# A recurrent attention with a gated feed-forward network on one core: raw weight words of the first units issued from ScalarE's queue, and the first load of x placed behind v

## The chip, the core and the metric

The kernel runs on 1 core of a Trainium2 chip. The metric is device time in microseconds (us), lower is better. Before the change it is 476.92 us (median of 3 runs, 476.25 to 478.91).

## The reference

Two blocks are computed one after the other, all in FP32 precision.

```python
# gated linear attention: B, H, S, D = 4, 8, 768, 48
for t in range(S):
    state = alpha[:, :, t, :, None] * state + einsum('bhd,bhe->bhde', k[:, :, t], v[:, :, t])
    y[:, :, t] = einsum('bhd,bhde->bhe', q[:, :, t], state)
# feed-forward: x is y as (3072, 384); w1, w2: (384, 1024); w3: (1024, 1024); w_out: (1024, 384)
a = x @ w1
b = x @ w2
out = ((a * b) @ w3) @ w_out
```

q, k, v and alpha are FP32. The four weights arrive as 64-bit floats, and the kernel reads them as raw 64-bit words and builds FP32 from them.

## The kernel before

**Chunks.** The sequence is cut into N = 24 chunks of C = 128 positions, six to a batch. A chunk n goes through these helpers, each named after what it makes:

- `load_a`, `load_kq`, `load_v` load alpha (192 KB), k and q (192 KB each) and v (192 KB). Their rows are 48 numbers, 192 bytes, long. Alpha and the pair of k and q have three buffers each, v has five.
- `logs` takes the logarithm of alpha on ScalarE (L272), `decays` sums it along the chunk on TensorE (L287) and takes two exponentials on ScalarE (L293, L294).
- `decayed` multiplies k and q by them on VectorE (L303, tile qk), `transposed` turns them on TensorE (L325) and copies them from PSUM on ScalarE (L327, tile qkT; two copies, the second is marked as ("qkT", n)).
- `scores` multiplies them on TensorE (L365) and masks the result on VectorE (L368, tile ms).
- `attend_state` (L385) and `attend` (L391) make the chunk's y on TensorE, ScalarE copies it (L395, tile x), and `store` writes it to a DRAM tensor xd on SP's queue in the next iteration (L262). `outer` (L337, then VectorE L345 or L347) and `advance` carry the state.

**Weight units.** w1 and w2 are converted in twelve units of 128 rows and 512 columns; the first six make the first half of the columns. A unit is a generator, `load_gates`, that calls `to_fp32`. Its first step loads 512 KB of raw words (L192; tile raw, four buffers, rows of 4 KB), the next ones convert: on ScalarE L200 (rest), L205 (power) and L217 (high part h), on VectorE L201, L204, L207, L208, L210 and L219 (low part l). `fetch(ahead)` takes first steps until `ahead` units are begun; `convert` does a fetch and then one further step of the oldest unit. `third` makes another part of a unit on TensorE (L233, L234) and ScalarE (L235).

**Gate.** Three chunks make a group. `load_x` reads a group's x back from xd (L407, tile xT, 576 KB), `split_x` splits it into three parts (ScalarE L413, VectorE L414 and L415), and `gate` multiplies the parts with those of the weights on TensorE (L421). The first group's split stands in iteration FIRST - 1 = 5, its matmuls begin in iteration 6. After the loop over chunks come the remaining gates, the folding of w3 with w_out, and the projection.

**What sets the order.** Each engine works through its own list in order, and so does each queue of DMA issues. Instructions are placed on the lists by the program's text and by the tile framework's scheduler; `after_marks(name)` holds what is issued inside it behind the marked instruction in that placement. Before the change all loads and stores of this stage are issued on SP's queue, the small transfers of the ends of chunks on POOL's. The transfers of SP take eight semaphores in turn, so a transfer waits for the one eight places before it to have landed; transfers issued by ScalarE take part in the same turn.

The loop over chunks begins so, before the change:

```python
    for n in range(N + 1):
        store()
        if n in loads:
            load_x(loads[n])
        load_a(n + 5)
        raws = (3, 3, 3, 3, 2, 2, 3, 3)[n] if n < 8 else 4
        for m in (n + 3,) * (n <= FIRST) + (n + 4,) * (n >= FIRST):
            load_kq(m)
            if n < FIRST - 2:
                fetch(raws)
            load_v(m - 1)
```

So the raw words of a unit lie on SP's queue between q and v of a chunk, and in iteration 4 `load_x(0)` stands behind the loads of that iteration.

Of the kernel before, what the change touches and what calls it, by code (L numbers as in the profile page):

```python
# [48 lines left out]
def kernel(  # L49
# [12 lines left out]
    nc = tc.nc  # L62
    B, H, S, D = q.shape
# [7 lines left out]
    KM = DM // C  # L71
# [31 lines left out]
    def bank():  # L103
        return ps.tile([C, 512], FP32, tag="bank", name="bank")

    st, mark = {}, {}

    def after_marks(*names):
        stack = ExitStack()
        for x in names:  # L110
            stack.enter_context(tc.issue_after(mark[x]))
        return stack
# [12 lines left out]
    def rows(src, n):  # L125
        b, c = divmod(n, NCH)
        return src[b, :, ds(c * C, C), :].rearrange("h p d -> p h d")
# [13 lines left out]
    def load_v(n):  # L141
        if n < N:
            st["v", n] = vs[n % len(vs)]
            nc.sync.dma_start(out=st["v", n][:, :, 0:D], in_=rows(v, n))

    nc.scalar.preload_act_table_set(LN_EXP_SET)
    load_a(0)
# [36 lines left out]
    for x in Ts + decs:  # L184
        nc.gpsimd.memset(x, 0.0)

    def to_fp32(dst, *srcs):

        n, m = len(srcs) * srcs[0].shape[1], srcs[0].shape[1]
        raw = rawp.tile([C, n], I64, tag="raw", name="raw")  # L190
        for i, src in enumerate(srcs):
            nc.sync.dma_start(out=raw[:, ds(i * m, m)], in_=src)  # L192
        yield
        words = raw.bitcast(U32).rearrange("p (n w) -> p n w", w=2)
        low, high = words[:, :, 0], words[:, :, 1]

        mant = cvt.tile([C, n], FP32, tag="mant", name="mant")
        top = mant.bitcast(U32)
        rest = cvt.tile([C, n], FP32, tag="rest", name="rest", bufs=2)
        nc.scalar.activation(rest, low, AF.Copy, scale=2.0 ** -52)  # L200
        nc.vector.tensor_scalar(top, high, 0x000FFFFF, 0x00100000, op0=ALU.bitwise_and, op1=ALU.bitwise_or)  # L201

        power = cvt.tile([C, n], U32, tag="power", name="power", bufs=2)
        nc.vector.tensor_scalar(power, high, 20, 0x7FF, op0=ALU.logical_shift_right, op1=ALU.bitwise_and)  # L204
        nc.scalar.activation(power, power, AF.Relu, scale=2.0 ** 23, bias=rebias)  # L205
        yield
        nc.vector.scalar_tensor_tensor(mant, top, 2.0 ** -20, rest, op0=ALU.mult, op1=ALU.add)  # L207
        nc.vector.scalar_tensor_tensor(power, high, 0x80000000, power, op0=ALU.bitwise_and, op1=ALU.bitwise_or)  # L208
        to = mant if dst is None else dst()
        nc.vector.tensor_mul(to, mant, power.bitcast(FP32))  # L210
        yield
        return to
# [24 lines left out]
    def fetch(ahead=3):  # L237
        while weights and len(begun) < ahead:
            begun.append(weights.popleft())
            next(begun[-1])  # L240
# [17 lines left out]
    def store():  # L258

        while later:  # L260
            dst, src = later.popleft()
            nc.sync.dma_start(out=dst, in_=src)  # L262
# [51 lines left out]
    def transposed(n):  # L314
        if n >= N:
            return
        qk = qks[n % 3]
        qkT = work.tile([C, 2, NP, C], FP32, tag="qkT", name="qkT")

        tp = [bank().rearrange("p (i j c) -> p i j c", i=2, j=NP) for _ in range(2)]  # L320
        for i in range(2):
            for j in range(NP):
                for half in range(2):
                    s = ds(DP * half, DP)
                    nc.tensor.transpose(tp[half][:, i, j, :], qk[s, i, 2 * j:2 * j + 2, :], ident[s, s])  # L325
        for half in range(2):
            mark["qkT", n] = nc.scalar.copy(qkT[:, :, :, ds(DP * half, DP)], tp[half]).ins  # L327
        st["qkT", n] = qkT
# [76 lines left out]
    def load_x(g, queue=nc.sync):  # L405
        st["xT", g] = xp.tile([C, KM, TG], FP32, tag="xT", name="xT")
        queue.dma_start(out=st["xT", g], in_=xd[g].rearrange("(k p) t -> p k t", p=C))  # L407
# [176 lines left out]
    with after_marks(("e", 0)):  # L584
        logs(1)
    decays(1)
    fetch(1)
    load_a(3)
    load_kq(2)
    decayed(1)  # L590
    fetch(2)
    load_v(1)
    load_a(4)


    FIRST = 6
# [3 lines left out]
    for n in range(N + 1):  # L600
        store()
        if n in loads:
            load_x(loads[n])
        load_a(n + 5)
        raws = (3, 3, 3, 3, 2, 2, 3, 3)[n] if n < 8 else 4
        for m in (n + 3,) * (n <= FIRST) + (n + 4,) * (n >= FIRST):
            load_kq(m)
            if n < FIRST - 2:
                fetch(raws)
            load_v(m - 1)  # L610
        if n:
            attend_state(n - 1)
        if n < N:
            scores(n)
        transposed(n + 1)
        if n - 2 in begin and n > FIRST:
            g, tiles = begin[n - 2]
            with after_marks(("ms", n), ("qkT", n + 1)):
                split_x(g, 0)
            fill.extend(gate(g, f) for f in tiles)  # L620
        pieces = (3, 3, 2, 0)[(n - FIRST) % 4] if n >= FIRST else 0
        if n == 0:
            with after_marks(("qkT", 0)):
                logs(2)
            decays(2)
            with after_marks(("e", 2)):
                logs(3)
        early, ready = n < FIRST, len(thirds) if n > 2 else n // 2
        marks = (*[("qkT", n + 1)] * (n < N - 1), *[("qk", n + 1), ("ms", n)] * early, *["x3"] * (n - 2 in begin and n > FIRST))
        if n < N - 2:  # L630
            with after_marks(*marks):
                convert(2 if n == 0 else 1, raws)
        advance(n)
        if n:
            attend(n - 1)
        outer(n)
        third(ready)
        run(pieces > 0)
        if early:
            with after_marks(*marks):  # L640
                convert(1, raws)
        with after_marks(*[("ms", n)] * (n < 3)):
            decayed(n + 2)
        if not early:
            with after_marks(*[("qkT", n + 1)] * (n < N - 4)):
                logs(n + 4)
        if n == 4:
            load_x(0)
        convert(early and n > 0, raws)
        run(pieces > 1)  # L650
        decays(n + 3)
        if early:
            with after_marks(("e", n + 3)):
                logs(n + 4)
        if n < N - 2:
            convert(early or n % 3 == 0, raws)
        if n == FIRST - 1:
            assert len(done) == 2 * KM
            g, tiles = begin[n - 2]
            with after_marks("l"):  # L660
                split_x(g, 0)
            fill.extend(gate(g, f) for f in tiles)
        run(pieces > 2)
        if n == N - 3:
            while begun:
                convert(1)
            weights.extend(load_out(j) for j in range(KF))
            fetch(4)
# [91 lines left out]
```

## Time and profile before

| what | value |
|---|---|
| median of the runs (range) | 476.92 us (476.25 to 478.91) |
| the profiled execution | 479.25 us |
| its span | 477.5 us |
| TensorE busy (PE) | 460.6 us, 96% |
| VectorE busy (DVE) | 359.4 us, 75% |
| ScalarE busy (ACT) | 279.4 us, 59% |
| GpSimd busy (POOL) | 71.2 us, 15% |
| raw words of w1, w2, w3 (L192), SP's queue | 28 transfers of 512 KB, median 5.3 us to landing |
| alpha, k, q, v, SP's queue | 24 transfers each of 192 KB, median 5.1, 5.2, 5.3 and 4.3 us to landing |

Every time inside the profile counts from the start of the span and belongs to the one profiled execution. Line numbers (L192) are those of the kernel before. PE is TensorE's matmul, PEld its loading of the stationary operand, SPq the queue of DMA issues of SyncE. The granted clock is TensorE's, as a share of full speed. The share of busy time over the whole span says little about the change, since it lies in the first 70 us or so; views that are cut to stretches are the ones to read.

### The profile page before, as it was taken

To read this page: it belongs to the slowest core of one execution; us is meant where nothing else is said; L and a number is where in the kernel's file an instruction comes from. 1 tells how busy PE (TensorE), PEld (TensorE's weight loads), DVE (VectorE), ACT (ScalarE), POOL (GpSimd) and SP (SyncE) were. 2 spreads that over 40 slices of the span, in tenths; PEclk is the share of its full clock that TensorE was granted. 3 is DMA by queue.
4 is the path that set the end of the run, shared out by engine and by line. 5 is a ranking of instruction groups with operands and counts; after the bars stand their busy time and mean duration, and the time that the engine had idled before them with its cause. 6 is when DMAs were issued, how large, how long until landed. Compare 5 with 4: busy or idle time off the path is not lost.

```text
span 477.5 us, 10025 instructions
## 1 busy us (share of the span) xinstructions
PE 460.6 (96%) x3836; PEld 435.6 (91%) x3836; DVE 359.4 (75%) x578; ACT 279.4 (59%) x555; POOL 71.2 (15%) x139
## 2 busy tenths in 40 slices
PE   4988899999999999999999999999999999999996
PEld 2766689889999998999999999999999999999996
DVE  2789677899969878899999968945542876666761
ACT  4668655768658554898877675654543533333330
POOL 3313112104202220112221201211011000000000
PEclk9999879999999999999999999999999999999999
DMA  9899999999899965467776532203012985555611
GB/s 170 184 205 206 226 203 264 197 220 202 191 227 202 215 190 150 130 211 227 224 243 188 172 138 84 97 37 100 33 51 70 267 244 173 167 168 173 179 51 49
DMA packets 153663, 80.29 MB, mean 168 GB/s; under 512 B 104480, under 2 KB 145696, under 8 KB 153616
## 3 DMA queue, kind: packets, MB, share of 16 engines
q1 hardware_dynamic: 148160, 65.42, 55.8%
q0 software_dynamic: 5456, 14.24, 9.3%
q8 instruction: 30, 0.49, 0.5%
q14 instruction: 17, 0.14, 0.1%
HBM read 57.58 MB, written 22.06 MB: 167 GB/s over the span
## 4 chain that ended last, share of the span: by engine, by line
PE 90%; DVE 3%; DMA 3%; ACT 2%; issue 1%; SPq 1%; DVEq 0%; ACTq 0%
PE bank L421 71%; PE bank L365 4%; PE bank L391 4%; PE bank L325 2%; PE bank L385 2%; PE bank L337 2%; PE bank L287 2%; PE bank L523 1%; DMA v<-in_v_dram 1%; PE bank L290 1%; DMA kq<-in_q_dram 1%; DVE qk L303 1%; DMA ac<-in_alpha_dram 1%; DVE power L208 0%; DVE mant L207 0%
## 5 line engine op out<-in xcount | busy, mean ns | idle before, releaser
L421 PE MATMUL bank<-x,w 128*128 128x384 f32 x1152 | 215.4, 341 | 1.1 <-ACT x L413 1.0
L421 PEld LDWEIGHTS bank<-x,w 128*128 128x128 f32 x1152 | 202.3, 190 | 4.8 <-ACT x L413 1.4
L421 PE MATMUL bank<-w3o,ab 128*128 128x384 f32 x576 | 100.2, 336 | 0.0
L421 PEld LDWEIGHTS bank<-w3o,ab 128*128 128x128 f32 x576 | 99.9, 188 | 0.0
L446 ACT ACTIVATE bank<-bank 128x384 f32<-128x384 f32 x96 | 45.7, 476 | 41.6 <-PE bank L421 41.4
L430 ACT ACTIVATE t<-bank 128x384 f32<-128x384 f32 x64 | 31.6, 495 | 63.3 <-PE bank L421 62.2
L496 POOL DMA_DIRECT2D abd<-ab x45 | 25.5, 566 | 145.1 <-DVE ab L482 126.3
L482 DVE TENSOR_TENSOR ab<-bank,r 128x384 f32<-128x384 f32 x44 | 24.4, 555 | 25.2 <-ACT bank L446 15.4
L552 DVE TENSOR_TENSOR ab<-abl,ab 128x1024 fp32r<-128x1024 f32 x24 | 29.4, 1225 | 12.8 <-ACT ab L551 12.8
L327 ACT COPY qkT<-bank 128x512 f32<-128x512 f32 x48 | 26.0, 594 | 22.0 <-PE bank L325 22.0
L551 ACT ACTIVATE ab<-abl 128x1024 fp32r<-128x1024 f32 x24 | 25.5, 1061 | 20.3 <-PE bank L421 17.9
L421 PE MATMUL bank<-wo,w3T 128*128 128x384 f32 x192 | 35.9, 334 | 0.0
L421 PEld LDWEIGHTS bank<-wo,w3T 128*128 128x128 f32 x192 | 33.5, 188 | 0.0
L368 DVE TENSOR_TENSOR ms<-bank,keep 128x512 int32<-128x512 int32 x48 | 31.3, 684 | 0.9 <-PE bank L365 0.8
L303 DVE TENSOR_TENSOR qk<-kq,e 128x768 f32<-128x768 f32 x24 | 23.2, 968 | 11.0 <-ACT e L294 8.8
L432 DVE SCALAR_TENSOR_TENSOR r<-bank,t 128x384 f32<-128x384 f32 x40 | 22.2, 555 | 12.1 <-PE bank L421 6.0
L365 PEld LDWEIGHTS bank<-qkT 48*128 48x128 f32 x384 | 24.9, 199 | 6.2 <-issue 3.4
L205 ACT ACTIVATE power<-power,rebias 128x512 uint32<-128x512 uint32 (+1 forms) x36 | 25.1, 699 | 9.0 <-DVE power L204 8.9
L432 DVE SCALAR_TENSOR_TENSOR o<-bank,t 128x384 f32<-128x384 f32 x24 | 13.4, 558 | 22.4 <-issue 13.7
L365 PE MATMUL bank<-qkT 48*128 48x128 f32 x384 | 29.7, 297 | 0.0
L553 DVE SCALAR_TENSOR_TENSOR ab<-ab,abl 128x1024 fp32r<-128x1024 f32 x24 | 29.3, 1219 | 0.0
L391 PE MATMUL bank<-ms,v 128*64 128x128 f32 x384 | 27.6, 288 | 0.0
(80 smaller groups left out, 574.9 us busy)
## 6 DMA issues: line engine op xcount, KB each, us to landing
raw<-in_moe_w_dram SPq DMA_DIRECT2D x28, 512.0 KB, 5.3
abl<-abd SPq DMA_DIRECT2D x24, 512.0 KB, 4.5
abd<-ab POOLq DMA_DIRECT2D x45, 192.0 KB, 3.1
xT<-xd POOLq DMA_DIRECT2D x9, 576.0 KB, 4.6
ac<-in_alpha_dram SPq DMA_DIRECT2D x24, 192.0 KB, 5.1
kq<-in_k_dram SPq DMA_DIRECT2D x24, 192.0 KB, 5.2
kq<-in_q_dram SPq DMA_DIRECT2D x24, 192.0 KB, 5.3
v<-in_v_dram SPq DMA_DIRECT2D x24, 192.0 KB, 4.3
```

The source lines that it names most:

```text
L303: mark["qk", n] = nc.vector.tensor_mul(qks[n % 3][:, :, :, 0:D], st.pop(("kq", n)), st.pop(("e", n)).rearrange("p i (h d) -> p i h d", h=H ...
L327: mark["qkT", n] = nc.scalar.copy(qkT[:, :, :, ds(DP * half, DP)], tp[half]).ins
L365: nc.tensor.matmul(sc[i][:, j, :], qkT[r, 0, j, :], qkT[r, 1, j, :], start=True, stop=True)
L368: masked = nc.vector.tensor_tensor(ms[:, i].bitcast(I32), sc[i].bitcast(I32), keep_bc, op=ALU.bitwise_and)
L391: nc.tensor.matmul(to, vc[:, 2 * j + i, :], ms[:, i, j, :], start=(n % NCH == 0 and j % HP == 0), stop=(j % HP == HP - 1), skip_group_chec ...
L421: nc.tensor.matmul(p, w[part][i], x[part][i], start=start and part == parts[0] and i == 0, stop=stop and part == parts[-1] and i == n - 1, ...
L430: nc.scalar.activation(t, p1, AF.Copy, scale=(1.0 + 1.0 / P) * scale)
L432: nc.vector.scalar_tensor_tensor(to, p2, scale, t, op0=ALU.mult, op1=ALU.add)
L446: nc.scalar.activation(p, p, AF.Copy, scale=1.0 + 1.0 / P)
L496: (nc.gpsimd if late else nc.sync).dma_start(out=abd[g][:, f, :], in_=ab)
L552: nc.vector.tensor_sub(t[:, 1], ab, t[:, 0].bitcast(FP32))
L553: nc.vector.scalar_tensor_tensor(t[:, 2], t[:, 0].bitcast(FP32), -1.0 - 1.0 / P, ab, op0=ALU.mult, op1=ALU.add)
```

## The change

Four things are edited.

1. `to_fp32` issues the raw words of the first 2 * KM = 6 units on ScalarE's queue; all later ones stay on SP's.
2. The fetches are placed elsewhere. The first stands behind the marked exponential of chunk 1 (it stood on SP's queue ahead of alpha of chunk 3), and `fetch(2)` before the loop is gone. In the loop, iterations 0 to 4 fetch behind the copies of qkT of chunk n + 1, where iterations 0 to 3 fetched between q and v.
3. `raws`, the number of units that may be begun, is 2 and not 3 in iterations 0 to 3.
4. `load_x(0)` in iteration 4 is held behind the last load of v.

```diff
     def load_v(n):
         if n < N:
             st["v", n] = vs[n % len(vs)]
-            nc.sync.dma_start(out=st["v", n][:, :, 0:D], in_=rows(v, n))
+            mark["v"] = nc.sync.dma_start(out=st["v", n][:, :, 0:D], in_=rows(v, n)).ins
...
+    fetched = []
+
     def to_fp32(dst, *srcs):
 
         n, m = len(srcs) * srcs[0].shape[1], srcs[0].shape[1]
         raw = rawp.tile([C, n], I64, tag="raw", name="raw")
+        fetched.append(n)
         for i, src in enumerate(srcs):
-            nc.sync.dma_start(out=raw[:, ds(i * m, m)], in_=src)
+            (nc.scalar if len(fetched) <= 2 * KM else nc.sync).dma_start(out=raw[:, ds(i * m, m)], in_=src)
         yield
...
     decays(1)
-    fetch(1)
+    with after_marks(("e", 1)):
+        fetch(1)
     load_a(3)
     load_kq(2)
     decayed(1)
-    fetch(2)
     load_v(1)
     load_a(4)
...
-        raws = (3, 3, 3, 3, 2, 2, 3, 3)[n] if n < 8 else 4
+        raws = (2, 2, 2, 2, 2, 2, 3, 3)[n] if n < 8 else 4
         for m in (n + 3,) * (n <= FIRST) + (n + 4,) * (n >= FIRST):
             load_kq(m)
-            if n < FIRST - 2:
-                fetch(raws)
             load_v(m - 1)
         if n:
             attend_state(n - 1)
         if n < N:
             scores(n)
         transposed(n + 1)
+        if n < FIRST - 1:
+            with after_marks(("qkT", n + 1)):
+                fetch(raws)
...
         if n == 4:
-            load_x(0)
+            with after_marks("v"):
+                load_x(0)
```

## The prediction

> **What bounds the kernel now.** I read the page first: TensorE (PE) is busy 96% of the span, so time can only be gained where PE idles or runs at a lower clock. The table by stretches of 10 us (columns: length, busy time of PE, weight load, VectorE, ScalarE, POOL, then PE clock, DMA share, GB/s) says where that is.
>
> ```profile
> 20.00:30.00 10.00, 9.52 (x138) 8.01 (x137) 8.47 (x15) 7.18 (x15) 3.64 (x7) 1.00 1.00 183
> 30.00:40.00 10.00, 8.58 (x122) 6.21 (x120) 8.49 (x15) 7.51 (x17) 2.17 (x4) 1.00 0.91 213
> 40.00:50.00 10.00, 7.76 (x117) 6.10 (x118) 9.17 (x17) 8.09 (x18) 2.03 (x5) 0.94 1.00 213
> 50.00:60.00 10.00, 7.97 (x89) 5.42 (x89) 6.31 (x10) 6.82 (x16) 1.88 (x3) 0.84 1.05 214
> 60.00:70.00 10.00, 9.89 (x65) 8.54 (x66) 7.17 (x13) 4.53 (x10) 1.43 (x4) 0.71 0.99 203
> 70.00:80.00 10.00, 10.00 (x140) 9.46 (x135) 9.37 (x16) 6.31 (x16) 1.72 (x3) 1.00 1.03 257
> ```
>
> The reader is to see that from 70 us on PE is full, so whatever is gained before 70 us is kept to the end, and that before it three resources are near their limit together: the DMA share is 0.9 to 1.05, VectorE is at 8.5 to 9.2 of 10, PE loses its time to both. From 20 to 60 us PE lacks 0.48 + 1.42 + 2.24 + 2.03 = 6.2 us. Next, the waits of 18 to 68 us (engine line, releaser: us in total, times, longest):
>
> ```profile
> PE bank L325 <- DVE qk L303: 3.1, 3, 1.6
> DVE qk L303 <- DMA kq<-in_q_dram: 2.2, 3, 1.2
> DVE w L219 <- ACT w L217: 2.2, 2, 1.4
> PE bank L337 <- DMA v<-in_v_dram: 2.0, 3, 1.2
> PE bank L421 <- ACT x L413: 1.0, 1, 1.0
> ```
>
> VectorE waits for q, PE for v, and PE for what VectorE makes of q. Then the timeline of SP's queue and the chain of waits, for where q and v stand and how the first gate matmul (L421) comes to start:
>
> ```profile
> 27.01 1.23 SPq L139
> 28.24 0.05 issue
> 28.29 0.99 SPq L192
> 29.28 0.04 issue
> 29.33 6.28 DMA v<-in_v_dram
> ...
> 54.32 0.69 DVE ms L368
> 55.01 0.88 DVE qk L303
> 55.88 0.14 issue
> 56.02 0.73 PE bank L325 x16
> 56.76 0.04 issue
> 56.79 1.07 ACT qkT L327 x2
> 57.87 1.07 ACT x L413
> 58.96 1.37 DVE x L414
> ```
>
> SP issues q, then raw words of a weight unit (L192), then v, and v lands 6.28 us later. The last stretch is serial: mask, qk of chunk 7, transposes, their copies, the split of x on ScalarE, the split on VectorE, and only then the gate. The xT load was issued at 50.70 and landed 5.8 later, at 56.5: it was there 1.2 us before ScalarE took it, so the order on ScalarE (behind the copies of qkT of chunk 7) set the start, not the load.
>
> [...]in slices of 1 us the granted clock is 0.50 from 49 to 52 us and 0.50 to 0.57 from 59 to 66 us[...], each after idle PE.
>
> **The change part by part.**
>
> (a) Six raw issues leave SP's queue: 1.01, 0.71, 0.78, 0.99, 0.63 and 1.68 us, 5.80 in sum, of a queue that issues without a break from 0.74 to 63 us. The instruction order of the changed kernel shows what that moves: v of chunk 3 is SP's 21st transfer and not its 25th, q of chunk 4 its 20th and not its 23rd, k, q, v of later chunks stand a group further ahead of the stores of x. So q's wait on VectorE (2.2 us, on VectorE which is 85 to 92% busy there) should go. I take 2.0. What is late next: VectorE itself. From the table its busy time between 20 and 50 us is 26.1 of 30 us, so at most 3.9 us are there to be had. The wait for v (2.0) lies on PE while VectorE was working (no gap on VectorE from 31.55 to 41.05), so its going is worth nothing by itself.
>
> (b) Each raw issue now stands on ScalarE, behind the copies of qkT and ahead of the unit's L200 and L205. ScalarE is busy 22.8 of the 30 us from 20 to 50. Per issue I take SP's mean, 5.80/6 = 0.97 us. Beside the iteration at 36 us: the copies end at 36.33, L200 would then end at 37.98 and L205 at 38.70, while VectorE took their results at 37.73 (L207) and 38.34 (L208): 0.25 to 0.36 late; in the changed order VectorE has a qk product (0.96) in between in most iterations, which hides it. I take 0.2 for each of six, 1.2 us. Below: 0, if the product always covers. Above: SP's issues of k and q took up to 3.27 us each[...]; six of these are 19.6 us against 7.2 us of free ScalarE time. The issue also waits for the transfer eight issues back; those are a chunk older and should have landed.
>
> (c) The lead of the raw words. Now a unit is issued after qkT of chunk n+1 and used one iteration later. In the timeline the copies end at 22.8, 29.0, 36.3, 42.5 and the first use on VectorE (L201) of the next unit is at 29.29, 36.61, 43.35, 49.33: a lead of 6.5 to 7.6 us against a landing of 4.8 to 6.7. It fits, with 0 to 1 us to spare if iterations shrink to VectorE's own some 6.2 us (qk 0.96, masks 2 x 0.68, T 0.35, unit 3.5). Cost taken: 0; bounds 0 to 1 us in each of five.
>
> (d) The start of the gate. In the changed order ScalarE splits x before it copies qkT of chunk 7, and VectorE makes qk of chunks 7 and 8 before it ends unit 5. That takes away PE's gap before L325 at 54.97 (1.05 us) and its wait for the split (1.0 us): 2.0 us. The xT load now stands behind one more a and k, but no raw words are in SP's queue, and the stores of x before it were held up there (x of chunk 2 was copied at 38.8, its store issued at 45.27). I take xT as landed in time; bound: 384 KB more ahead of it, at the 185 GB/s of the slices with small rows only, is 2.1 us later, which would eat it all.
>
> (e) The clock. From 58.98 to 68.09 (L365 of chunk 7) PE needed 9.1 us for 27 gate matmuls and one L287 pair; the same set at full clock, 18 in 3.41, 9 in 1.72 and the pair in 0.51, is 5.6. So 3.5 us are lost there to half clock and starts of the split. [...]Bounds 0 and 3.5; I take 1.4, a little under half[...].
>
> Sum: 2.0 + 2.0 + 1.4 - 1.2 = 4.2 us less. The profiled execution took 479.25 (span 477.5, and 1.75 around it), so it would be 475.05; the median of the runs is 476.92, so I forecast 472.7.
>
> After 70 us both kernels do the same work, and the six later units stay on SP; PE has 10.0 of 10 there, so I expect neither gain nor loss.
>
> **The rivals.**
>
> 1. Forecast, 0.45: 472.7 (469.5 to 474.5, from 2.4 to 7 us gained).
> 2. The clock stays full over the start of the gate as well: 2.0 + 2.0 + 3.5 - 1.2 = 6.3 us, 470.6. For it: five shorter gaps on PE. Against: PE's work per iteration is about 5.3 of 6.2 us. 0.15.
> 3. The transfer is the bound anyway. No byte is saved, the DMA share is about 1.0 from 2 us on, and xT has more in front of it. Then q and v come earlier only at the price of raw words and xT, and the gate starts where it did: 2 us gained early, 1 to 2 lost: 476. For it: the share. Against: the share falls to 0.3 to 0.7 in single slices (22 to 25, 34 to 36, 45 to 46, 53 to 55 us), so there is room. 0.18.
> 4. Slower: ScalarE is held at the raw issue, at L192's new place, [...]by the transfer eight back. It decides from about 1.7 us an issue, where the 1.2 us of (b) have become the 5 that are gained. At 2.5 us an issue, five issues that lie on the path at 2.5 - 0.97 + 0.2 = 1.7 each are 8.7 us, less 4 gained and with unit 5 late at the gate: 481. For it: k and q issues of 3.2 us, [...]and everything behind the issue on ScalarE (L200, L205, copies of x, the exponentials that the next qk needs) waits, with PE and VectorE behind these. Against: SP's raw issues[...] took 1.0 on average. 0.22.
>
> **How the numbers follow.** What a measurement of this kernel can tell from no change is about 0.5%, 2.4 us. Cases 1 and 2 are faster (0.60), case 3 is the same (0.18), case 4 slower (0.22). The range goes from the far side of case 2 (467.5: q's 2.2, v's 2.0, 2.0 and 3.5 in full, at no cost, are 9.7 us, to 467.2) through case 3 and into the near part of case 4 (479.5); the forecast's own range is 469.5 to 474.5.
>
> **What would show it.** Right: raw issues on ScalarE near 1 us; no wait of qk for q between 18 and 50 us; ScalarE's split of x ahead of the copies of qkT of chunk 7; the first L421 at 54 to 56 us instead of 58.98; L365 of chunk 7 at 62 to 66 instead of 68.09. Wrong: ScalarE issues of 2 us and more, or VectorE waiting at L201 for raw words, or L421 waiting for xT; and any gap of PE after 70 us would break the step that keeps the gain.

## The result and the profile after

| | before | after |
|---|---|---|
| median of 10 runs | 477.30 us | 480.13 us |
| range | 476.25 to 478.91 | 479.28 to 481.23 |
| profiled execution, its span | 479.25, 477.5 | 481.23, 479.4 |
| scores of chunk 7 on TensorE start (L365, now L368) | 68.09 | 69.92 |

The ratio is 1.0056, 95% interval 1.0041 to 1.0071: slower by about 2.7 us, where 4.2 less were forecast. Lines of the changed kernel stand three higher in number (raw words L195, rest L203, high part L220, low part L222, split of x L416 to L418, gate L424).

First the table of stretches of the changed kernel, with the columns named in the prediction.

```profile
20.00:30.00 10.00, 7.82 (x101) 6.29 (x98) 8.09 (x16) 6.11 (x14) 2.73 (x5) 0.83 1.11 191
30.00:40.00 10.00, 7.82 (x84) 6.42 (x83) 6.53 (x11) 4.96 (x11) 2.78 (x6) 0.66 0.96 187
40.00:50.00 10.00, 8.65 (x123) 6.62 (x121) 7.27 (x14) 7.23 (x17) 1.85 (x4) 1.00 0.97 203
50.00:60.00 10.00, 8.70 (x117) 6.91 (x116) 7.13 (x13) 9.19 (x20) 1.67 (x4) 0.83 0.96 242
60.00:70.00 10.00, 9.36 (x32) 7.60 (x32) 8.36 (x14) 5.38 (x12) 2.00 (x5) 0.66 1.06 195
70.00:80.00 10.00, 10.00 (x131) 9.46 (x133) 9.05 (x16) 5.21 (x12) 1.51 (x3) 1.00 0.86 229
```

From 20 to 40 us TensorE does 15.64 us of work (18.10 before), ScalarE 11.07 (14.69) and VectorE 14.62 (16.96): the stage has become emptier on TensorE, VectorE and ScalarE, while the share of the DMA engines is as high as before (1.11 and 0.96, before 1.00 and 0.91). From 70 us on TensorE is full, as before; over 70 to 477 us it is busy 405.70 of 407 us. The 1.83 us by which the scores of chunk 7 are late are the whole difference of the two spans (1.9).

The waits between 18 and 72 us (engine line, releaser: us in total, times, longest):

```profile
ACT rest L203 <- DMA ac<-in_alpha_dram: 11.7, 4, 5.3
DVE mant L210 <- ACT rest L203: 4.1, 4, 1.7
DVE T L350 <- POOL T L359: 3.4, 1, 3.4
ACT rest L203 <- DMA raw<-in_moe_w_dram: 3.1, 1, 3.1
DVE qk L306 <- ACT qkT L330: 2.8, 1, 2.8
PE bank L237 <- DVE w L222: 1.9, 1, 1.9
```

The waits of VectorE for q and of TensorE for v that the prediction began with are gone. A new one is larger than both: ScalarE idle for 11.7 us at L203 for alpha. L203 doesn't read alpha, it reads raw words; so what waited stands ahead of it. The timeline of ScalarE shows what stands ahead of it (start, duration, in brackets the idle time before it and what ended it):

```profile
23.51 0.33 ACTq L195 DMA_DIRECT2D raw<-in_moe_w_dram  x1
23.89 0.66 ACT L203 ACTIVATE rest<-raw 128x512 f32<-128x512 uint32 x1 [2.24 <-DMA ac<-in_alpha_dram]
...
33.27 0.34 ACTq L195 DMA_DIRECT2D raw<-in_moe_w_dram  x1
33.70 0.67 ACT L203 ACTIVATE rest<-raw 128x512 f32<-128x512 uint32 x1 [5.35 <-DMA ac<-in_alpha_dram]
```

An issue of raw words takes 0.33 us, but it starts only when an alpha has landed, and L203 is behind it. Below, such an issue is called held. The chain of waits says the same (start, duration, what):

```profile
17.67 5.82 DMA ac<-in_alpha_dram
23.49 0.02 issue
23.51 0.33 ACTq L195
...
25.15 8.09 DMA ac<-in_alpha_dram
33.24 0.02 issue
33.27 0.34 ACTq L195
```

Why alpha: in the changed kernel one iteration puts seven transfers into the turn of eight semaphores: k, q, v, two stores of x, one alpha, and the raw words right behind that alpha. The transfer eight places before a raw issue is therefore the alpha of the iteration before. It was still on its way: the two alphas above took 5.82 and 8.09 us from issue to landing, and the two raw issues start 0.02 us after they landed.

The holds are not all that VectorE waits for. Of ScalarE's 11.7 us only 4.1 us show up as waits of VectorE for L203 (L210 in the list above). During the longest hold VectorE stands idle 3.4 us for something else, for POOL, which multiplies the carried state T by a decay. From the timelines of POOL and of VectorE:

```profile
25.36 1.42 POOL L314 DMA_DIRECT2D dec<-ends  x2 [4.56 <-DMA ends<-e]
31.39 0.20 POOL L357 TENSOR_TENSOR dec<-dec 128x4 f32<-128x4 f32 x1 [4.10 <-DMA dec<-ends]
31.95 0.51 POOL L359 TENSOR_TENSOR T<-tmp,dec 128x192 f32<-128x192 f32 x1
32.48 0.36 DVE L350 TENSOR_TENSOR T<-bank,T 128x192 f32<-128x192 f32 x1 [3.41 <-POOL T L359]
```

Before, POOL made this T at 29.30 and nobody waited for it. The small transfer of e that it needs left POOL's queue at 16.30 then; in the changed kernel it stands behind one that waits for an alpha and leaves at 20.32, before any hold. So this is a second delay, beside the holds.

Last, the timeline of VectorE at the start of the gate, first before the change, then after it:

```profile
53.71 0.69 DVE L219 SCALAR_TENSOR_TENSOR w<-w,mant 128x512 fp32r<-128x512 f32 x1 [1.43 <-ACT w L217]
58.96 1.36 DVE L414 TENSOR_TENSOR x<-xT,x 128x1152 fp32r<-128x1152 f32 x1 [1.22 <-ACT x L413]
```

```profile
55.50 0.69 DVE L213 TENSOR_TENSOR mant<-mant,power 128x512 f32<-128x512 f32 x1
59.00 0.96 DVE L306 TENSOR_TENSOR qk<-kq,e 128x768 f32<-128x768 f32 x1 [2.81 <-ACT qkT L330]
59.88 0.68 DVE L222 SCALAR_TENSOR_TENSOR w<-w,mant 128x512 fp32r<-128x512 f32 x1
60.48 0.68 DVE L371 TENSOR_TENSOR ms<-bank,keep 128x512 int32<-128x512 int32 x1
61.08 1.35 DVE L417 TENSOR_TENSOR x<-xT,x 128x1152 fp32r<-128x1152 f32 x1
```

The last instruction of unit 5 (L222) starts at 59.88 (this start is called unit 5's end below); before, it (L219) started at 53.71, and the split of x on VectorE (58.96) waited for ScalarE's split. Now the split of x (61.08) stands behind unit 5. A third delay is the idle 2.81 us ahead of the product of chunk 8. They are put down to a copy of qkT; the q of chunk 8 landed at 58.9, which fits as well. It was issued at 55.29, before the change at 55.20, so it is no later than it was; but before the change VectorE made this product at 63.62, behind the split, and now it needs it ahead of unit 5's end.

The chain of waits from there to the gate (start, duration, what):

```profile
48.21 4.66 DMA xd<-x
...
52.92 4.38 DMA xT<-xd
...
58.39 0.58 ACT qkT L330
...
59.88 0.70 DVE w L222
60.57 0.04 issue
60.62 0.80 PE bank L237
61.41 2.40 PE bank L424 x6
```

The gate (L424) stands on TensorE behind L237, which makes the third part of unit 5 and waits 1.9 us for L222: the gate needs unit 5 itself, and not only the split. Behind L222 the chain goes back through ScalarE's split to xT and to the store of x.

### The profile page after: what moved, and what is told of

It reads as the page before. It is cut to its first block, busy times and chain, and to the rows that moved or that the text cites. A ratio compares the mean times of both kernels' runs of the same rounds, so it can differ in the third digit from the quotient of the medians.

```text
span 479.4 us, 10014 instructions
## 1 busy us (share of the span) xinstructions
PE 460.2 (96%) x3836; PEld 437.2 (91%) x3836; DVE 358.4 (75%) x578; ACT 279.0 (58%) x555; POOL 70.9 (15%) x139
## 4 chain that ended last, share of the span: by engine, by line
PE 90%; DMA 7%; ACT 1%; issue 1%; DVE 1%; SPq 0%; ACTq 0%; DVEq 0%
PE bank L424 71%; PE bank L394 4%; PE bank L368 4%; DMA ac<-in_alpha_dram 4%; PE bank L328 2%; PE bank L388 2%; PE bank L340 2%; PE bank L526 1%; PE bank L293 1%; DMA raw<-in_moe_w_dram 1%; PE bank L290 1%; DMA xd<-x 1%; DMA xT<-xd 1%; ACT power L208 0%; PE bank L237 0%
## 5 line engine op out<-in xcount | busy, mean ns | idle before, releaser
L424 PE MATMUL bank<-x,w 128*128 128x384 f32 x1152 | 215.2, 341 | 0.1
L424 PEld LDWEIGHTS bank<-x,w 128*128 128x128 f32 x1152 | 202.6, 190 | 3.4 <-issue 0.9
L424 PE MATMUL bank<-w3o,ab 128*128 128x384 f32 x576 | 100.2, 336 | 0.0
L424 PEld LDWEIGHTS bank<-w3o,ab 128*128 128x128 f32 x576 | 99.9, 188 | 0.0
L424 PE MATMUL bank<-wo,w3T 128*128 128x384 f32 x192 | 35.9, 334 | 0.0
L203 ACT ACTIVATE rest<-raw 128x512 f32<-128x512 uint32 (+1 forms) x36 | 23.2, 645 | 19.1 <-DMA ac<-in_alpha_dram 11.7
L424 PEld LDWEIGHTS bank<-wo,w3T 128*128 128x128 f32 x192 | 33.5, 188 | 0.0
L435 DVE SCALAR_TENSOR_TENSOR r<-bank,t 128x384 f32<-128x384 f32 x40 | 22.0, 553 | 11.7 <-PE bank L424 7.5
L368 PEld LDWEIGHTS bank<-qkT 48*128 48x128 f32 x384 | 25.1, 198 | 5.7 <-issue 3.0
L368 PE MATMUL bank<-qkT 48*128 48x128 f32 x384 | 29.9, 297 | 0.0
L208 ACT ACTIVATE power<-power,rebias 128x512 uint32<-128x512 uint32 (+1 forms) x36 | 25.1, 697 | 6.7 <-DVE power L207 6.3
```

The costliest lines, as they stand in the source:

```text
L368: nc.tensor.matmul(sc[i][:, j, :], qkT[r, 0, j, :], qkT[r, 1, j, :], start=True, stop=True)
L424: nc.tensor.matmul(p, w[part][i], x[part][i], start=start and part == parts[0] and i == 0, stop=stop and part == parts[-1] and i == n - 1, ...
L435: nc.vector.scalar_tensor_tensor(to, p2, scale, t, op0=ALU.mult, op1=ALU.add)
```

## The experiments

All are compared with the kernel before on the same chip. Three theories: A, ScalarE is held at its raw issues until the transfer eight back has landed. B, the raw words are asked for too late, since one unit fewer is begun ahead. C, xT in front of q of chunk 8 on SP's queue makes the gate late. POOL's T was no theory of its own, and no run takes that wait alone away; it is absent in e1, e6 and e17 below, which lose as much as the change.

**First round: parts of the change.**

e1, the changed kernel with its raw words on SP's queue:

```diff
-            (nc.scalar if len(fetched) <= 2 * KM else nc.sync).dma_start(out=raw[:, ds(i * m, m)], in_=src)
+            nc.sync.dma_start(out=raw[:, ds(i * m, m)], in_=src)
```

> The changed kernel, with the raw words of the first six units back on SP's queue; the new places of the fetches and raws = 2 stay. Theory A (ScalarE is held at its own issue of raw words until the transfer eight places back, an alpha load of SP's, has landed): ScalarE's idle time ahead of L203 with alpha as releaser, 11.7 us in the changed kernel, falls below 2 us, and the time to 476 to 478 us, at least 2 us under the changed kernel. Theory B (the raw words are asked for too late, with one unit fewer ahead; the queue does not matter): VectorE waits for raw words, and the time stays at 479 to 481 us.

480.84 us, ratio 1.0064 (1.0036 to 1.0091). ScalarE's wait for alpha is gone and the loss stays; VectorE now waits 6.4 us for raw words (L204) and ScalarE 3.8 (L203). So A is not needed for a loss of this size.

e2, only units 0 and 1 on ScalarE:

```diff
-            (nc.scalar if len(fetched) <= 2 * KM else nc.sync).dma_start(out=raw[:, ds(i * m, m)], in_=src)
+            (nc.scalar if len(fetched) <= 2 else nc.sync).dma_start(out=raw[:, ds(i * m, m)], in_=src)
```

> The changed kernel, but only the first two units' raw words go by ScalarE's queue; units 2 to 5 by SP's. In the changed kernel ScalarE had no long wait at the first two issues and 2.2, 5.3, 1.8 and 2.4 us at the next four. Theory A: these four waits go and the time is 475 to 478 us. Theory B: 479 to 481 us, since the units are asked for as late as before.

477.79 us, ratio 1.0002 (0.9986 to 1.0018): the loss is gone with the four held issues, though ScalarE still waits 6.7 us and VectorE 5.1 us for raw words. That speaks for A, against e1. It isn't the holds alone, though: in e2 VectorE makes the product of chunk 8 at 60.19, behind the split of x (57.38), and in the change ahead of it, so the third delay went too.

e3, the first load of x on POOL's queue:

```diff
-            with after_marks("v"):
-                load_x(0)
+            load_x(0, nc.gpsimd)
```

> The changed kernel, but the load of x of the first group is issued on POOL's queue, so that q of chunk 8 no longer stands behind it on SP's. Theory C (the gate starts late because SP is held 2.9 us at the load of x until the last store of x has landed, so q of chunk 8 is late and with it VectorE's list): VectorE's wait of 2.8 us before qk of chunk 8 goes, the first gate matmul comes 1.5 to 2.8 us earlier than 61.3 us, and the time is 477 to 478.5 us. Theory A alone: the four waits of ScalarE are still 11 to 12 us, and the time stays within 1 us of the changed kernel's 480.

482.91 us, ratio 1.0116 (1.0088 to 1.0143): slower than the change itself. ScalarE waits 3.2 us for xT. VectorE waits 6.1 us for raw words, those of the seventh unit: its first instruction (60.27) now stands ahead of unit 5's last (62.75). As a remedy C fails; since VectorE's order changed with it, it doesn't test C cleanly.

e4, the kernel before with nothing but the other queue: places and number of units as before.

```diff
-            nc.sync.dma_start(out=raw[:, ds(i * m, m)], in_=src)
+            (nc.scalar if len(fetched) <= 2 * KM else nc.sync).dma_start(out=raw[:, ds(i * m, m)], in_=src)
```

> The kernel before, with one edit: the first six units' raw words are issued by ScalarE, where the order of before puts them (no marks, raws = 3). The first four issues stand at the very start of ScalarE's list, ahead of the loads of later chunks, the last two among its work with a transfer eight back. Theory A: ScalarE is held at the last two only, up to 5 us in all; four raw units early delay the first chunks by 2 to 5 us, so 478 to 482 us. Theory B: the units are asked for early here, so no loss, 473 to 477 us.

479.02 us, ratio 1.0028 (1.0017 to 1.0039). Nothing holds the places any more: four of the issues come at 0.8 to 8.8 us, and with these 2 MB ahead the first chunks are late (VectorE's first two products of q and k start at 9.77 and 16.80 us, before at 7.13 and 11.78). It says little on A or B.

**Second round: queue and lead apart.** Here `raws` is the number of units that may be begun in iterations 0 to 3: 3 before, 2 in the change.

e5 is e1 with three units; e7 is the changed kernel (raw words on ScalarE) with three:

```diff
-        raws = (2, 2, 2, 2, 2, 2, 3, 3)[n] if n < 8 else 4
+        raws = (3, 3, 3, 3, 2, 2, 3, 3)[n] if n < 8 else 4
```

> The changed kernel with its raw words back on SP's queue (as in e1) and with raws 3 and not 2 in iterations 0 to 3, so one unit more is begun ahead; on SP's queue only the raw words move against e1. Theory B (raw words asked for too late): the waits of VectorE (L204) and ScalarE (L203) for raw words, 9.4 us together in e1, fall below 3 us, scores of chunk 7 start near 67.5 to 69, time 477 to 478.5. Theory A (only the hold of ScalarE costs): nothing here was held in e1 either, so the time stays at e1's 480.8.

477.75 us, ratio 1.0001 (0.9987 to 1.0015). On SP's queue the longer lead takes the whole loss of e1 away.

> The changed kernel with raws 3 in iterations 0 to 3, all six raw words still on ScalarE's queue: two are issued together behind qkT of chunk 1, each later one an iteration ahead of where it was. Theory A: each issue still stands on ScalarE behind a transfer eight back; ScalarE's idle time for alpha at L203 (11.7 us in the changed kernel) stays above 6 us, time 479 to 481. Theory B: with the longer lead the time is that of e5, 477 to 478.5.

483.90 us, ratio 1.0132 (1.0109 to 1.0155). The longer lead makes it worse on ScalarE. Its timeline of ScalarE:

```profile
17.00 0.33 ACTq L195 DMA_DIRECT2D raw<-in_moe_w_dram  x1
17.38 0.49 ACT L296 ACTIVATE e<-bank 128x384 f32<-128x384 f32 x1 [3.10 <-DMA v<-in_v_dram]
...
26.83 0.33 ACTq L195 DMA_DIRECT2D raw<-in_moe_w_dram  x1
27.21 0.68 ACT L203 ACTIVATE rest<-raw 128x512 f32<-128x512 uint32 x1 [2.88 <-DMA kq<-in_k_dram]
...
37.30 0.34 ACTq L195 DMA_DIRECT2D raw<-in_moe_w_dram  x1
37.69 0.66 ACT L203 ACTIVATE rest<-raw 128x512 f32<-128x512 uint32 x1 [6.00 <-DMA v<-in_v_dram]
```

Every held issue has v or k in the brackets now, since the turn has another order: 3.10 + 2.88 + 6.00 and a fourth of 2.63 are 14.6 us of idle ScalarE, with no wait for raw words of note (1.4 us up to 72 us). VectorE waits 12.1 us for L203 between 18 and 72 us, where it was 4.1 in the change: here the hold reaches it almost whole. ScalarE waits another 5.2 us for xT. So the hold costs with the longer lead too; e7 against e5 is 6 us, though SP's list differs between the two in some loads of alpha as well. B alone falls here.

e6, the kernel before with the short lead alone, and without the `fetch(2)` ahead of the loop:

```diff
-    fetch(2)
...
-        raws = (3, 3, 3, 3, 2, 2, 3, 3)[n] if n < 8 else 4
+        raws = (2, 2, 2, 2, 2, 2, 3, 3)[n] if n < 8 else 4
```

> The kernel before with only the shorter lead: raws 2 and not 3 in iterations 0 to 3, and no fetch(2) ahead of the loop; raw words stay between q and v on SP's queue. Theory B: waits for raw words at L200 and L201 of 5 us or more in all, 479.5 to 481. Theory A: no hold on ScalarE, so the time of the kernel before, 477.3 +- 0.7.

479.98 us, ratio 1.0051 (1.0031 to 1.0071): with no hold at all, a short lead and a late second unit cost the kernel before as much as the change does.

e8, raw words on POOL's queue, held in place by a copy of one column on POOL:

```diff
-            with after_marks(("qkT", n + 1)):
+            with hold(st["qkT", n + 1][:, 0, 0, C - 1:C]):
                 fetch(raws)
```

> The changed kernel with the six raw words on POOL's queue, each held behind a one-column copy of qkT (of e for the first) on POOL, so that they are asked for at the same place and ScalarE isn't held. Theory A: ScalarE's idle time for alpha at L203 is gone, 477 to 479. Theory B: the lead is as short as in the changed kernel and in e1, so VectorE and ScalarE wait for raw words 5 us or more, 480 to 481.

484.88 us, ratio 1.0155 (1.0133 to 1.0178). ScalarE isn't held, but POOL's own waits delay the issues (37.91, 42.50, 49.14 for units 3 to 5), and the waits for raw words are 18.8 us up to 72 us. About 2.2 us of it are lost behind the scores of chunk 7, as with the added tile of e14 below (this kernel adds one too). It fits B and says nothing on A.

**Third round: the hold alone, and the gain alone.**

e9, e5 with a load of 32 bytes issued by ScalarE where the change issues raw words:

```diff
             with after_marks(("qkT", n + 1)):
+                nc.scalar.dma_start(out=tick[n:n + 1], in_=alpha[0, 0, 0:1, 0:8])
                 fetch(raws)
```

> e5 (raw words on SP's queue, three units ahead, SP's order unchanged) with one load of 32 bytes more per iteration, issued on ScalarE behind the copies of qkT where the changed kernel issues raw words; nobody reads what it loads. Theory A (ScalarE held at an issue until the transfer eight back landed): ScalarE stands idle in front of these issues 8 us or more in all between 18 and 60 us, and the time rises from e5's level by 2 to 6 us, to 480 to 484, though no raw word is late. Theory B (only the late raw words cost): the little loads cost their issue alone, five times 0.34 us, and the time stays within 1 us of e5's 477.75.

482.24 us, ratio 1.0094 (1.0076 to 1.0113), but not by A: in its timeline no issue is held (none has a wait for a load ahead of it), and unit 5 ends at 54.52. By the count of the turn that had to be so: with one more transfer per iteration the turn has eight, as in e13 below, and no alpha lies eight back. The scores of chunk 7 start at 67.92, in e5 at 65.63; from there to the end it takes 412.7 us, in e5 409.5. The second part is mostly the added tile, as e14 shows. As a test of A it failed.

e10, the kernel before with two lines exchanged, so that v goes ahead of the raw words; the lists of the other engines are unchanged:

```diff
-            if n < FIRST - 2:
-                fetch(raws)
             load_v(m - 1)
+            if n < FIRST - 2:
+                fetch(raws)
```

> The kernel before with only two lines swapped: in iterations 0 to 3 the raw words stand behind v and not ahead of it on SP's queue; all other engines keep their order. Step (a) of the prediction, without its price: the waits for v on TensorE (2.0 us before) go and VectorE's wait for q stays about as it was, 476 to 477.5. If v and q were covered anyway: 477.5 +- 0.7.

477.63 us, ratio 0.9999 (0.9989 to 1.0010). The wait for v leaves the list of waits, and the time doesn't move.

e11, e2 with three units, so without hold and without short lead (against the changed kernel):

```diff
-            (nc.scalar if len(fetched) <= 2 * KM else nc.sync).dma_start(out=raw[:, ds(i * m, m)], in_=src)
+            (nc.scalar if len(fetched) <= 2 else nc.sync).dma_start(out=raw[:, ds(i * m, m)], in_=src)
...
-        raws = (2, 2, 2, 2, 2, 2, 3, 3)[n] if n < 8 else 4
+        raws = (3, 3, 3, 3, 2, 2, 3, 3)[n] if n < 8 else 4
```

> The changed kernel with only units 0 and 1 on ScalarE's queue (as in e2, where neither issue was held) and three units ahead as in e5. If both theories hold, both costs are away and something of the gain on q and v is left: no wait for raw words over 2 us, none of ScalarE for alpha at an issue, 475 to 477. If the early gain is given back at the gate in any case, 477.5 +- 0.7.

477.54 us, ratio 0.9990 (0.9976 to 1.0003). In the profiled execution the gate starts at 56.26 and the scores of chunk 7 at 63.5, 4.6 us earlier than before; the span is 476.7. From there to the end it takes 413.2 us, before 409.4. TensorE idles 1.6 us between 70 and 150 us and its granted clock is 0.82 from 116 to 124 us. In this execution 3.8 us were given back behind the scores of chunk 7.

e12, e10 with the second unit's raw words behind v as well:

```diff
     decayed(1)
-    fetch(2)
     load_v(1)
     load_a(4)
+    fetch(2)
```

> As e10, and the second unit's raw words too stand behind v of chunk 1 and one alpha, ahead of the loop. Theory B: unit 1 is asked for some 2 us later and every later unit stays, so the same as e10 within 1 us; if q and v of the first chunks matter, up to 1 us below it.

478.25 us, ratio 1.0011 (0.9998 to 1.0023): the same as e10 within the intervals.

**Fourth round: what was left open.**

e13, the change with one more small transfer per iteration, so that the turn has eight:

```diff
             load_v(m - 1)
+            if 0 < n < FIRST:
+                nc.sync.dma_start(out=turn[n:n + 1], in_=alpha[0, 0, 0:1, 0:8])
```

> The changed kernel with one transfer of 32 bytes more per iteration (1 to 5) on SP's queue, from DRAM to DRAM and read by nobody. It makes the turn of semaphores come round once per iteration: the raw words issued by ScalarE in iterations 2 to 4 now stand behind the raw words before them and not behind an alpha; all engines but SP keep their order up to the gate, and the lead is the short one. Theory A (ScalarE is held by the alpha eight back): the 11.7 us that ScalarE stood idle for alpha at L203 fall below 2 us, and the time falls from 480.1 to 477 to 478.5. Theory B alone (late raw words): the waits for raw words stay or grow and the time stays at 480 +- 0.7.

479.73 us, ratio 1.0045 (1.0033 to 1.0058). The hold for alpha is gone, as the turn of semaphores would have it; one of 3.5 us on the small transfer itself is left. The last unit is asked for at 41.56 instead of 47.77. But VectorE now waits 5.3 us for q, 4.2 of them at once, and unit 5 ends at 58.28. The 4.2 us are those of chunk 8: VectorE is ready for its product at 53.23, in the change at 56.19, and gets it at 57.40, when q has landed. So the explanation of the hold is borne out, and most of the 3.0 us that VectorE is earlier go into the third delay. How much of the loss the hold is, is not shown: the small transfers also changed SP's queue.

e14, e5 with e9's tile and nothing else:

```diff
+    nc.gpsimd.memset(const.tile([C, 8], FP32, name="tick"), 0.0)
     fetched = []
```

> e5 with a tile of 32 bytes per partition more in the pool of constants, set to zero once on POOL and read by nobody, as e9 had it (e8 had one of 4 bytes). If the place of the later tiles in SBUF is what made matmuls of the last 80 us come at 228 and not 233 per 40 us in e8 and e9: the same here, and 480 to 482. If e9's loss came from its five small loads: e5's time, 477.75 +- 0.7, and 233 per 40 us.

479.57 us, ratio 1.0050 (1.0033 to 1.0067). The stretches of e5, then of e14 (same columns):

```profile
390.00:430.00 40.00, 40.00 (x233) 40.00 (x232) 28.06 (x30) 14.65 (x20) 0.00 (x0) 1.00 0.59 177
430.00:470.00 40.00, 40.00 (x233) 40.00 (x232) 24.32 (x26) 12.70 (x17) 0.00 (x0) 1.00 0.37 116
```

```profile
390.00:430.00 40.00, 40.00 (x228) 40.00 (x227) 27.90 (x29) 14.15 (x19) 0.00 (x0) 1.00 0.58 176
430.00:470.00 40.00, 40.00 (x228) 40.00 (x227) 24.90 (x27) 13.40 (x18) 0.00 (x0) 1.00 0.36 115
```

With an unused tile of 32 bytes per partition 40 us hold 228 and not 233 of the long matmuls, at the same granted clock of 1.00. That is about half of what e9 lost; the other half lies before the scores of chunk 7 (67.92 against 65.63 in e5) and came with the five small loads.

e15, the kernel before where units 1 to 5 use the raw words of unit 0:

```diff
-        raw = rawp.tile([C, n], I64, tag="raw", name="raw")
-        for i, src in enumerate(srcs):
-            nc.sync.dma_start(out=raw[:, ds(i * m, m)], in_=src)
+        count[0] += 1
+        if 1 < count[0] <= 2 * KM:
+            raw = count[1]
+        else:
...
```

> The kernel before without the raw loads of units 1 to 5: these five units convert the raw words of unit 0 again, so their weights are not those of the reference; 2.5 MB of transfers and five issues on SP's queue are left out, all arithmetic stays. It bounds from above what any placing of the raw words can bring. If the early stage is bound by what the DMA engines move (rival 3), 2.5 MB at about 200 GB/s are 12 us of transfer and the gate starts several us earlier: 470 to 474. If VectorE and the serial work of the chunks bound it: 476 to 477.5, and then step (a) had nothing to gain wherever the raw words stand.

472.63 us, ratio 0.9892 (0.9876 to 0.9908): with 2.5 MB and five issues away, 5.2 us are gained. The scores of chunk 7 start at 61.70, and nothing is given back behind them (409.3 us to the end).

e16, the kernel before without L208 in the first six units:

```diff
-        nc.vector.scalar_tensor_tensor(power, high, 0x80000000, power, op0=ALU.bitwise_and, op1=ALU.bitwise_or)
+        count[0] += 1
+        if count[0] > 2 * KM:
+            nc.vector.scalar_tensor_tensor(power, high, 0x80000000, power, op0=ALU.bitwise_and, op1=ALU.bitwise_or)
```

> The kernel before without the merge of the sign (L208, 0.61 us each on VectorE) in the first six units, so their weights lose their sign; all transfers stay. If VectorE binds the early stage, 6 x 0.61 = 3.7 us less there bring 2 to 3.5 us: 474 to 475.5. If the transfers bind it: 477.5 +- 0.7.

477.59 us, ratio 0.9998 (0.9986 to 1.0011): 3.7 us less work on VectorE don't move the time. The trace, of a run near the median (477.35), says more. The scores of chunk 7 start at 63.82, earlier than before (68.09), than in e10 (66.46) and than in e5 (65.63); but from there to the end it takes 411.7 us, before 409.4. In this execution less work on VectorE did bring the gate forward, and 2.3 us of that were given back behind the gate. So e16 doesn't show that VectorE is no bound of the early stage.

e17, the kernel before with `raws` 2 and not 3, and nothing else (`fetch(2)` stays). Up to the gate, SP's list differs in one thing: units 2 to 5 come an iteration later.

```diff
-        raws = (3, 3, 3, 3, 2, 2, 3, 3)[n] if n < 8 else 4
+        raws = (2, 2, 2, 2, 2, 2, 3, 3)[n] if n < 8 else 4
```

> The kernel before with raws 2 and not 3 in iterations 0 to 3 and nothing else: fetch(2) ahead of the loop stays, so unit 1 is asked for at 13.5 us as before, and units 2 to 5 an iteration later, as in e6. In the changed kernel too, unit 1 is asked for at 13.51. If e6's loss came from the late second unit (17.56), and the late units 2 to 5 alone cost nothing (as e2 says): 477.5 +- 0.7, and then the changed kernel's loss is that of ScalarE's hold. If the late units 2 to 5 cost it: 479 to 480.5, as e6, and the changed kernel's loss can be the lead's alone.

480.64 us, ratio 1.0071 (1.0048 to 1.0095). Its timeline of VectorE at the gate:

```profile
54.79 0.42 DVE L201 TENSOR_SCALAR mant<-raw 128x512 uint32<-128x512 uint32 x1
...
59.56 0.69 DVE L219 SCALAR_TENSOR_TENSOR w<-w,mant 128x512 fp32r<-128x512 f32 x1 [0.69 <-ACT w L217]
60.17 1.35 DVE L414 TENSOR_TENSOR x<-xT,x 128x1152 fp32r<-128x1152 f32 x1
```

Unit 5 ends at 59.56, and the split of x starts the moment VectorE is through with it; before, the split of x waited 1.22 us for ScalarE, with unit 5's last instruction begun 5.2 us ahead of it. In e17 the waits for raw words add up to only 4.8 us between 18 and 60 us, in pieces of 1.4 at most, yet they and the shifted order move the last unit by 5.9 us.

**Put together.** The start of unit 5's last instruction (L219 or L222, 0.7 us long) and of VectorE's split of x are from one profiled execution each, the ratio from all runs. The profiled execution of the kernel before took 2.0 us more than the median of its runs, that of the change 1.1 us more than its own, so differences of a microsecond or two between traces say little.

| kernel | unit 5 ends | split of x | ratio |
|---|---|---|---|
| before | 53.71 | 58.96 | 1 |
| e5 (SP, three units) | 51.97 | 57.22 | 1.0001 |
| e10 (v first) | 52.59 | 57.83 | 0.9999 |
| e12 (v first, also for unit 1) | 53.02 | 58.28 | 1.0011 |
| e11 (two on ScalarE, three units) | 55.18 | 56.23 | 0.9990 |
| e2 (two on ScalarE) | 56.78 | 57.38 | 1.0002 |
| e13 (turn of eight) | 58.28 | 59.48 | 1.0045 |
| e6 (short lead) | 59.43 | 60.03 | 1.0051 |
| e17 (short lead, unit 1 in time) | 59.56 | 60.17 | 1.0071 |
| after | 59.88 | 61.08 | 1.0056 |
| e4 (queue alone) | 59.96 | 60.56 | 1.0028 |
| e1 (after on SP) | 60.35 | 60.96 | 1.0064 |
| e3 (xT on POOL) | 62.75 | 63.35 | 1.0116 |
| e7 (ScalarE, three units) | 65.94 | 66.54 | 1.0132 |

(The kernels with an added tile, e8, e9 and e14, are left out, and e15 and e16, which leave work out.) Where unit 5 ends by 56.8 us, nothing is lost, whatever the queue; where it ends from 58.3 us on, all lose, whatever the queue, though not in the order of the column. The traces say how: in the kernels that lose, the split of x stands right behind unit 5 on VectorE or one or two instructions later, and in most of them TensorE waits for unit 5 right before the gate (1.9 us in the change, 4.6 in e13, 1.9 to 2.9 in e1, e6 and e17). That would be what A, B and C have in common. No run moves unit 5 alone, so it is a reading of fourteen traces and not an experiment.

Behind the gate the kernels differ little: from the scores of chunk 7 to the end of the span it takes 409.3 to 409.8 us in all fourteen but e11 (413.2), and in e15; it is 411.7 in e16 and 411.7 to 412.7 in the three with an added tile.

## Why the prediction was wrong, step by step

- **(a), 2.0 us for the wait for q: the wait went, the gain did not come.** e5, e10 and e11 put v, or q and v, ahead of raw words, and their time is that of the kernel before: a wait that moves from q to raw words is the same bytes in another order. e15, which takes 2.5 MB away, gains 5.2 us. That fits rival 3, that the transfers bind the stage, but doesn't prove it: e15 also takes five issues from SP's queue. The step named VectorE as the next bound with 3.9 us to be had. e16 doesn't refute that: its gate came earlier and it lost the time behind it. A small slip: "no gap on VectorE from 31.55 to 41.05" passes over one of 0.19 us before 39.22.
- **(b), 1.2 us for the issues: the step that failed most plainly.** An issue takes 0.33 to 0.38 us on ScalarE, not 0.97; that term was too large. "The issue also waits for the transfer eight issues back; those are a chunk older and should have landed" is the sentence that failed: the turn was not counted out, and the wait was put at nothing. It gives an alpha, with a wait of 1.8 to 5.4 us in four of six issues, 11.7 us of ScalarE, of which 4.1 show up as waits of VectorE. e7 shows it again with v and k, e13 that another turn removes it.
- **(c), cost 0 for the lead: not settled.** Forecast were 6.5 to 7.6 us from the copies of qkT to the first use. In the trace units 2 to 5 have 6.7, 10.1, 6.7 and 6.8 us, as forecast. The holds of 1.3 to 4.9 us behind the copies leave 4.8, 5.2, 5.4 and 4.9 us from issue to first use (23.51 to 28.32, 33.27 to 38.49, 39.98 to 45.34, 47.77 to 52.64), which is about what the words need to land (4.5 to 6.4), and VectorE waits only 0.3 us for them. So in the changed kernel itself the short lead shows no cost of its own. On SP's queue it costs about 3 us (e1 against e5) and, with the order of the kernel before, 3.4 us (e17), but nothing in e2.
- **(d), 2.0 us at the gate: failed, with a cost that it didn't price.** The order came as foreseen: ScalarE splits x (57.32) before it copies qkT of chunk 7 (58.39), and VectorE makes the product of chunk 8 before it ends unit 5. But that order needs q of chunk 8 some 4.6 us earlier than before, and (d) put nothing down for it; VectorE stood 2.81 us. xT was not in time either: SP stood still from 50.04 to 52.92 until the store of x had landed, and issued xT 2.2 us later than before. ScalarE waits only 0.26 us for it, but the chain of waits to the gate goes through it. The first gate matmul came at 61.31 instead of 58.98.
- **(e), 1.4 us for the clock: it went the other way.** The 1.4 was the author's estimate between 0 and 3.5; how much of the low clock goes away with shorter gaps on TensorE, which rival 2 needs as well, wasn't shown. In the change the granted clock is 0.83 and 0.66 from 50 to 70 us against 0.84 and 0.71, and 0.66 from 30 to 40 us, where it was 1.00. Over the whole span it is 0.977 to 0.989 in the ten runs of the change and 0.985 to 0.996 in the 160 runs of the kernel before that stand beside the experiments. It goes with the time in e6: its five runs at 0.991 or more take 477.2 to 478.9 us, its other ten 479.4 to 482.8. Whether the clock is a cost of its own or follows from the idle TensorE before the gate isn't shown.
- **Behind 70 us: right** for this pair of kernels (TensorE full, the difference of the spans made before). In the executions of e11 and e16, which reach the gate earlier, it wasn't: part of what was gained before the gate was given back behind it.
- **A path that no step has:** POOL's T, 2.65 us later than before, for which VectorE stood 3.4 us.

Rival 4 named the hold by the transfer eight back, with unit 5 late at the gate, and its price, 481; it was given 0.22. That 480.13 was measured is in part luck: its sum has five issues of 2.5 us on the path, where four waits, 4.1 us in all, show up on VectorE and two other costs stand beside them. Its argument against itself, that SP's issues took 1.0 us on average, looked at how long an issue lasts, while what counts is what it waits for. The prediction's first sign of being wrong, "ScalarE issues of 2 us and more", missed for the same reason: the issues are short, and the wait stands before them.

What stays open: how the 2.7 us divide. No run takes POOL's T or the product of chunk 8 alone away. A hold costs with the longer lead (e7). The short lead costs without a hold in e1, e6 and e17, but not in e2, although e2 and e17 ask for their last unit at the same time (46.69 and 46.80). So either can be enough, and the short lead needn't be. No version that beats the kernel before with full work was found.

## What to carry to other kernels

When a DMA issue moves to a compute engine, count out which transfer's semaphore it takes over, and when that one lands: here four held issues held all of ScalarE's work for 11.7 us, and the profile booked the wait on the harmless instruction behind each. Before a wait is counted as a gain, take its bytes away in an experiment (e15) and its engine's work in another (e16), and read from the trace where the time went: an unchanged total can hide a gain that was given back later. Where an engine is held, see which other waits of the next engine lie in the same stretch (here POOL's T, 3.4 us): they may stay when the hold goes. And when an order brings a piece of work forward, ask when its inputs come.

## What was not expected of the hardware

- ScalarE issues 512 KB of raw words in 0.33 to 0.38 us. SP's next three issues of the same size in the same run (up to 68 us) took 0.42 to 1.19 us, before up to 1.68; over the whole run the median of SP's 22 is 0.33 us too, so what lengthens an issue in the early stage isn't SP as such.
- With a second issuing queue the DMA engines moved about as much: 202 GB/s over the first 70 us against 199 before, and from 20 to 40 us 191 and 187 against 183 and 213. What the second queue cost here is the hold, 11.7 us of idle ScalarE.
- With a tile of 32 bytes per partition that nobody reads the time is 0.5% longer (e14, ratio 1.0050, against e5, 1.0001): 40 us hold 228 and not 233 matmuls of 128x384, at a granted clock of 1.00 in both. What it is about the tile isn't shown.
